# Stores of x with rows outermost, and tokens on partitions in early numerators

## The chip, the core and the metric

The kernel runs on one core of one Trainium2 chip. The metric is the device time of one execution in microseconds (us). Five engines work side by side: TensorE (PE: matrix products, and PEld, its weight loads), VectorE (DVE), ScalarE (ACT), GpSimd (POOL) and SyncE (SP), which here issues almost all transfers. Sixteen transfer (DMA) engines move the data.

## The reference

```python
def phi(x):
    proj = einsum('bhsd,df->bhsf', x, w_phi)             # 64 -> 128 features
    proj = proj - max(abs(proj), axis=-1, keepdims=True)
    return concatenate([exp(proj), exp(-proj)], axis=-1)
q_p, k_p = phi(q), phi(k)                                # 8 batches, 8 heads, 576 tokens, 64
kv = einsum('bhsf,bhsd->bhfd', k_p, v)
z = sum(k_p, axis=2)
num = einsum('bhsf,bhfd->bhsd', q_p, kv)
den = einsum('bhsf,bhf->bhs', q_p, z)[..., None] + 1e-06
attn = num / den
x = attn.transpose(0, 2, 1, 3).reshape(4608, 512)        # tokens, heads * 64
g = x @ w_gate                                           # 512 -> 1536
y = (g * sigmoid(g) * (x @ w_val)) @ w_out               # 1536 -> 512
```

The second half (the gated layers) is by far the larger part of the products.

## The kernel before

**Attention.** `attention` works on pairs of heads: 32 pairs, four to a batch. For a pair it loads k, q and v by SP (L529 to L545), projects them on TensorE, takes the largest value and subtracts it on VectorE, applies the exponentials on ScalarE, sums keys times values into a bank of PSUM (L605, L598), copies that sum to SBUF, and forms numerators and denominators. Pairs 0 to 11 are the early ones. They run at the start, while the weights are taken apart: these come as 64-bit floats, and VectorE and ScalarE split each into a high and a low 32-bit part. Pairs 12 to 31 run later, beside the products of the gated layers.

**Two forms of numerators.** An early pair goes through `finish_early`: the products leave features on partitions and tokens along a row (L817, L821), the denominators of 32 rows each are turned, inverted, copied across partitions (L845) and turned back (L837 to L847), and one product scales the numerators (L849). They then lie as the gated layers want x: 128 partitions are two heads times 64 features. A late pair goes through `finish`: the products leave tokens on partitions (L764), 65 columns for each 64 tokens, the last of which is the denominator; VectorE inverts 9 columns, scales out of PSUM into `num` (L780) and turns blocks of 32 x 32 into `turned` (L786).

**x.** It is a matrix of 512 rows (four pairs of 128) by 4608 tokens, worked on in chunks of 384 tokens. For pairs 0 to 7, x goes straight into the tiles `xh` and `xl` (high and low part). From pair 8 on it is stored to `x_dram` by SP: by one transfer of `num` for an early pair (L858), and by four transfers of `turned` for every two late pairs (L798, twenty pairs, ten groups of four). It is loaded again into `stage` (L1166) or `x_kept` (L506).

**The gated layers.** `first` and `second` (products at L388) work on the first four chunks; their middle values go to `h_dram` and come back (L989, L994), and low parts of weights come from `wlo_dram` (L932, L942, L944). The other eight chunks go two at a time through `strassen` (products at L1218), with combined weights streamed from `wv_dram` and `wlo_dram` (L1152); `operands` first forms the combinations of x from `stage` (L1176 to L1182).

**The order.** No order is written by hand. Each piece of work is a step with an engine, a cost, the steps it needs and a rank; `Plan.run` plays them through and so fixes the order on every engine. Each engine then works through its own list in that order. A transfer costs SP 500 ns to issue there, and all transfers share one wire of 320 bytes per ns, whatever their form. Where TensorE would stand still in this play, `nothing` puts filler products on idle data (L1412 to L1417). SP issues in order, too: a transfer that has to wait holds back all that stand behind it, and each transfer waits for the one eight places ahead of it to have landed.

Of the kernel before, what the change touches and what calls it, by code (L numbers as in the profile page):

```python
# [9 lines left out]
F32 = mybir.dt.float32  # L10
# [275 lines left out]
def favor_attention_moe(ctx: ExitStack, tc: tile.TileContext, qT, kT, v, w_phi, wg, wv, wo, out):  # L286
# [37 lines left out]
    kvs = sb("kvs", [P, 4 * P], F32, 2)  # L324
    qx = [sb("qx0", [P, 2, S]), sb("qx1", [P, 2, S])]
    qe = sb("qe", [P, 2, S], F32, 2)
    num, den = sb("num", [P, S]), sb("den", [P, S])
# [3 lines left out]
    rc = sb("rc", [P, NBL])  # L331
# [4 lines left out]
    shared = [pool.tile([P, 2 * DM], dt, name=f"shared{i}", tag=f"shared{i}") for i, dt in enumerate((U32, U32, F32, F32))]  # L336
# [145 lines left out]
    turned_tiles = []  # L482

    def turned_tile(n, g):
        if not turned_tiles:
            turned_tiles.extend(pool.tile([P, 2, SH], F32, name=f"turned{m}", tag=f"shared{m}") for m in range(4))
        return turned_tiles[2 * n + g]
# [32 lines left out]
    def attention(i, rank):  # L520
# [14 lines left out]
        q_width = 4 * P if early else S  # L535
        q_in = [add("SP", P * q_width * 4, lambda: nc.sync.dma_start(qin[jq][:, :q_width], qT[b, pr, :, :q_width]), q_free, rank)]
        if early:
            q_in.append(add("SP", 2 * D * D * 4, lambda: nc.sync.dma_start(side(qin[jq]), ends(qT)), q_free, rank))
# [89 lines left out]
        sums = lambda: ps_kv()[:, :4 * VD].rearrange("p (s h d) -> p s h d", s=2, h=2)  # L628

        kv_sum = lambda: kvs[j][:, :2 * P].rearrange("p (s h d) -> p s h d", s=2, h=2)  # L630
        z_sum = lambda: kvs[j][:, 2 * P:3 * P].rearrange("p (s h r) -> p s h r", s=2, h=2)
        if early:
            kvc = [add("ACT", act(4 * D), lambda: nc.scalar.copy(kv_sum(), sums()[:, :, :, :D]), [kv_steps[-1], *use("kvs")], rank)]
            kvc.append(add("ACT", act(P), lambda: nc.scalar.copy(z_sum(), sums()[:, :, :, D:VD].broadcast_to([P, 2, 2, 32])),
                           kvc[:1], rank, give=("kv", i)))
        else:
            kvc = [add("ACT", act(4 * VD), lambda: nc.scalar.copy(kvs[j][:, :4 * VD], ps_kv()[:, :4 * VD]),  # L637
                       [kv_steps[-1], *use("kvs")], rank, give=("kv", i))]
# [5 lines left out]
        if early:  # L644
            for g in range(3):
# [42 lines left out]
                def exponential(k, g=g, tail=tail, key2=key2):  # L688
                    if tail:
                        x = work[plan.bank[key2]][:, :P].rearrange("p (h s) -> p h s", h=2)  # L690
                        o = (qe, qx)[k][j][:, :, 4 * P:]
                    else:
                        x, o = work[plan.bank[key2]][:, :4 * P], (qe, qx)[k][j][:, g, :4 * P]
                    nc.scalar.activation(o, x, AF.Exp, scale=-1.0 if k else 1.0)
# [59 lines left out]
        def finish(extra):  # L754
# [4 lines left out]
            def over():  # L759
# [8 lines left out]
            nu = add("PE", 2 * blocks_ * KV_PACE, over, [*f1, *kvc, *extra], rank,  # L768
# [14 lines left out]
                for part, at, m in parts_]  # L783
            n, r = i // 2 % 2, i % 2
            over_ = [*raw_free, *wa_free, *we_free] if i < EARLY_PAIRS + 4 else last["sent", i - r - 4]
            t3 = [add("DVE", dve(SH), lambda g=g: vec.transpose(  # L786
                turned_tile(n, g)[:, r].rearrange("p (n s) -> p n s", s=32), even[:, :, 32 * g:32 * g + 32]),
                [*normal, *over_], rank) for g in range(2)]
            last["turned", i] = t3[1]
# [6 lines left out]
            for h in range(2):  # L796
                for g in range(2):
                    sent.append(add("SP", D * S * 4, lambda h=h, g=g: nc.sync.dma_start(  # L798
                        x_dram[b - LATE_BATCH, (2 * h + g) * 32:(2 * h + g + 1) * 32, :, pr - 1:pr + 1].rearrange("j p r s -> p j (r s)"),
                        turned_tile(n, g)[h * D:(h + 1) * D].rearrange("p r s -> p (r s)")), t3, rank))  # L800
# [4 lines left out]
        def finish_early(extra):  # L805
            features = lambda k, h, c: (qe, qx)[k][j][:, h, c]
            free = last.get(("num", i - 1), ())
            main, tail = slice(0, 4 * P), slice(4 * P, S)
            TAIL = S - 4 * P

            def over():
                low, high = (work[plan.bank[key]] for key in (("d", i), ("n", i)))
                for k in range(2):
                    for h in range(2):
                        for part, c in enumerate(halves):
                            at = 32 * (2 * h + part)
                            nc.tensor.matmul(low[at:at + 32, :SH], z_sum()[:, k, h], features(k, h, c), start=k == 0, stop=False)  # L817
                for o, c, first_ in ((low[:, SH:SH + TAIL], tail, False), (high, main, True)):
                    for k in range(2):
                        for at in range(0, P, 32):  # L820
                            nc.tensor.matmul(o[at:at + 32], kvs[j][:, k * P + at:k * P + at + 32], features(k, at // D, c),  # L821
                                             start=first_ and k == 0, stop=k == 1)

            nu = add("PE", 2 * pe32(SH) + 2 * (60 + pe32(4 * P)), over, [f1, *kvc, *extra], rank,
                     take=[("d", i), ("n", i)], mode="quarters")
            dn = add("ACT", act(SH), lambda: nc.scalar.activation(
                den[:, :SH], work[plan.bank["d", i]][:, :SH], AF.Copy, bias=1e-6), [nu, *free], rank)
            copied = [add("ACT", act(TAIL), lambda: nc.scalar.copy(
                num[:, tail], work[plan.bank["d", i]][:, SH:SH + TAIL]), [nu, dn, *free], rank, give=("d", i))]
            copied.append(add("ACT", act(4 * P), lambda: nc.scalar.copy(  # L830
                num[:, main], work[plan.bank["n", i]]), [nu, *free], rank, give=("n", i)))
            last["kvs", i] = last["nu", i] = last["qe", i] = last["qx", i] = nu

            wide = lambda t: t.rearrange("p (a j) -> p a j", j=32)
            NH = NBL // 2
            turned = den[:, SH:]
            t0 = add("DVE", dve(SH), lambda: vec.transpose(turned, den[:, :SH]), [dn], rank)  # L837
            t1 = add("DVE", 260, lambda: vec.reciprocal(
                rc.rearrange("p (g a) -> p g a", g=2),
                wide(turned)[:, :, 0:1].rearrange("p a o -> p o a").broadcast_to([P, 2, NH])), [t0], rank)  # L840
            crossed = []
            for h in range(2):
                for part in range(2):
                    r, q = (slice(32 * (2 * h + g), 32 * (2 * h + g) + 32) for g in (1 - part, part))
                    crossed.append(add("ACT", 200, lambda r=r, q=q, part=part: nc.scalar.copy(  # L845
                        rc[r, part * NH:(part + 1) * NH], rc[q, part * NH:(part + 1) * NH]), [t1], rank))
            t2 = add("DVE", dve(S), lambda: vec.transpose(  # L847
                wide(den), rc.rearrange("p (a o) -> p a o", o=1).broadcast_to([P, NBL, 32])), crossed, rank)
            t3 = add("DVE2", dve(S), lambda: vec.tensor_tensor(out=num, in0=num, in1=den, op=ALU.mult), [t2, *copied], rank)  # L849
            last["rc", i] = t2  # L850


            read_num = []
            for c, at, start, width in cuts:
                src = num[:, start:start + width]
                if b >= LATE_BATCH:
                    if not read_num:
                        read_num.append(add("SP", P * S * 4, lambda: nc.sync.dma_start(  # L858
                            x_dram[b - LATE_BATCH, :, :, pr], num.rearrange("p (u s) -> p u s", u=2)), [t3], rank))
                    x_kept.setdefault(c, []).extend(read_num)  # L860
                    continue
                dst = lambda x, c=c, at=at, width=width: x[c % X_SETS][:, pr, at:at + width]
                hi = add("ACT", act(width), lambda src=src, dst=dst: nc.scalar.copy(dst(xh), src),
                         [t3, *x_free.get(c - X_SETS, ())], rank)
                lo = pair_op("POOL" if early else "DVE2", width, lambda dst=dst: dst(xl), src, lambda dst=dst: dst(xh),
                             ALU.subtract, [hi], rank)
                x_ready.setdefault((c, pr), []).extend([hi, lo])
                read_num.extend([hi, lo])
                if i < BANK_PAIRS:
                    early_done.extend([hi, lo])  # L870
            last["num", i] = read_num
# [598 lines left out]
```

## Time and profile before

| | us |
|---|---|
| median of 3 runs (range) | 1231.64 (1229.57 to 1232.07) |
| profiled execution: time | 1231.18 |
| profiled execution: span | 1229.4 |
| TensorE busy | 1172.2 (95%) |
| VectorE busy | 793.4 (65%) |
| ScalarE busy | 545.3 (44%) |
| GpSimd busy | 140.9 (11%) |

The mean granted clock of TensorE is 0.978 of full speed. The transfers move 298.32 MB, 243 GB/s over the span. Busy time of TensorE is an upper bound of its work: ends of products are modelled, and products at a lower clock are longer. A wait is put down to the engine or transfer that came last by the profile; a chain of such waits has to be followed to where it starts.

### The profile page before, as it was taken

The numbers are of one execution on the slowest core, as the hardware profiler recorded it, in microseconds if no ns is written. First come the engines' busy times: TensorE is split into PE (matmuls) and PEld (weight loads), VectorE is DVE, ScalarE is ACT, GpSimd is POOL, SyncE is SP. The second block draws the span as 40 slices with busy tenths as digits, with TensorE's granted clock in tenths as the row PEclk, the third lists the DMA queues.
The fourth block names the chain that finished last, engine by engine and source line by source line (L and its number), as shares of the span: only waits on it lengthen the run. The fifth ranks groups of instructions, "written<-read, shape, count | busy, mean of one in ns | idle before, by whom it ended". The sixth has DMA issues, their size and how long they took to land. (4 is left out here: it accounts for less than half of the span.)

```text
span 1229.4 us, 26393 instructions
## 1 busy us (share of the span) xinstructions
PE 1172.2 (95%) x9978; PEld 1026.6 (84%) x9978; DVE 793.4 (65%) x1593; ACT 545.3 (44%) x1233; POOL 140.9 (11%) x142
## 2 busy tenths in 40 slices
PE   9999999999999889998979899997999999799998
PEld 7777889999888768987967789896699897599986
DVE  7998899997567637676756255785345785434441
ACT  6887543333435435453534243553333553333332
POOL 1323200000132212010100001110001110001100
PEclk9999999999999989998989899998999999899999
DMA  5656778777999779986766688866688767779864
GB/s 162 175 162 186 247 249 288 249 254 234 333 310 303 253 253 339 344 240 201 242 189 184 198 283 285 241 211 212 221 270 286 238 213 221 244 233 309 281 200 160
DMA packets 220031, 298.32 MB, mean 243 GB/s; under 512 B 65280, under 2 KB 125824, under 8 KB 219904
## 3 DMA queue, kind: packets, MB, share of 16 engines
q1 hardware_dynamic: 219744, 296.56, 75.4%
q8 instruction: 79, 1.29, 0.5%
q14 instruction: 48, 0.39, 0.1%
q10 hardware_dynamic: 160, 0.07, 0.0%
HBM read 217.91 MB, written 78.64 MB: 241 GB/s over the span
## 5 line engine op out<-in xcount | busy, mean ns | idle before, releaser
L388 PE MATMUL work<-w_hi,hh 128*128 128x512 f32 x468 | 187.7, 409 | 24.6 <-ACT hh L1006 16.7
L381 DVE TENSOR_TENSOR m<-m,hh 128x384 fp32r<-128x384 f32 x132 | 74.8, 573 | 140.1 <-ACT hh L1006 122.1
L388 PE MATMUL work<-w_hi,m 128*128 128x512 f32 x396 | 160.6, 405 | 0.9 <-DVE m L381 0.9
L1240 DVE TENSOR_TENSOR m<-m,work 128x384 f32<-128x384 f32 x144 | 78.5, 552 | 121.9 <-ACT m L1237 73.2
L1006 ACT CAST hh<-m 128x384 fp32r<-128x384 f32 x144 | 73.1, 512 | 182.8 <-DMA m<-h_dram 92.3
L381 POOL TENSOR_TENSOR m<-m,m 128x384 f32<-128x384 f32 x48 | 58.4, 1216 | 646.3 <-DVE m L1245 365.3
L388 PE MATMUL work<-xh,w_big 128*128 128x384 f32 x384 | 132.3, 345 | 0.0
L388 PEld LDWEIGHTS work<-w_hi,hh 128*128 128x128 f32 x468 | 90.4, 193 | 48.0 <-ACT hh L1006 18.6
L388 PE MATMUL work<-xl,w_big 128*128 128x384 f32 x384 | 128.6, 335 | 0.0
L1218 PE MATMUL work<-tb,stream_xh 128*128 128x384 f32 x618 | 115.3, 338 | 0.0
L1218 PEld LDWEIGHTS work<-tb,stream_xh 128*128 128x128 f32 x618 | 107.0, 188 | 4.7 <-issue 3.8
L1237 ACT COPY m<-work 128x384 f32<-128x384 f32 x144 | 68.1, 474 | 79.2 <-PE work L1218 71.5
L1218 PE MATMUL work<-tb,stream_xl 128*128 128x384 f32 x468 | 90.8, 343 | 9.1 <-ACT m L1237 9.1
L1244 ACT ACTIVATE m<-m 128x384 f32<-128x384 f32 x96 | 45.4, 517 | 111.4 <-DVE m L1240 111.3
L388 PEld LDWEIGHTS work<-w_hi,m 128*128 128x128 f32 x396 | 76.5, 193 | 20.5 <-DVE m L381 2.4
L1218 PEld LDWEIGHTS work<-tb,stream_xl 128*128 128x128 f32 x468 | 82.7, 191 | 12.7 <-ACT m L1237 9.5
L588 ACT ACTIVATE kp<-kp 128x512 f32<-128x512 f32 x128 | 78.2, 630 | 24.4 <-DVE kp L583 23.2
L1218 PE MATMUL work<-tb,tb 128*128 128x384 f32 x408 | 79.3, 341 | 4.6 <-ACT m L1237 4.6
L388 PEld LDWEIGHTS work<-xh,w_big 128*128 128x128 f32 x384 | 72.2, 188 | 7.7 <-issue 4.8
L1218 PEld LDWEIGHTS work<-tb,tb 128*128 128x128 f32 x408 | 71.8, 191 | 7.5 <-ACT m L1237 4.9
L381 POOL TENSOR_TENSOR s<-s 128x256 f32<-128x256 f32 x48 | 43.1, 897 | 282.4 <-DMA s<-w_dram 250.4
L388 PE MATMUL work<-w_lo,hh 128*128 128x512 f32 x183 | 74.1, 405 | 0.0
(141 smaller groups left out, 2345.8 us busy)
## 6 DMA issues: line engine op xcount, KB each, us to landing
stream_xh<-wv_dram SPq DMA_DIRECT2D x103, 256.0 KB
h_dram<-m SPq DMA_DIRECT2D x124, 192.0 KB
m<-h_dram SPq DMA_DIRECT2D x124, 192.0 KB
stream_xl<-wv_dram SPq DMA_DIRECT2D x78, 256.0 KB
tb<-wv_dram SPq DMA_DIRECT2D x77, 256.0 KB
w_lo<-wlo_dram SPq DMA_DIRECT2D x72, 256.0 KB
stream_w_lo<-wv_dram SPq DMA_DIRECT2D x52, 256.0 KB
stream_xl<-wlo_dram SPq DMA_DIRECT2D x48, 256.0 KB
```

The costliest lines, as they stand in the source:

```text
L381: (nc.gpsimd if on == "POOL" else nc.vector).tensor_tensor(out=o, in0=a, in1=b, op=op)
L388: nc.tensor.matmul(o, l, r, start=a, stop=z)
L588: nc.scalar.activation(kpv[:, :m2, s], kpv[:, :m2, 1], AF.Exp, scale=-1.0 if s else 1.0)
L1006: s4 = add("ACT", act(CH), lambda: nc.scalar.copy(hh[b], th(j)), [made, hid_free[b]], FIRST)
L1218: nc.tensor.matmul(o(), l, r, start=begin and k + m == 0, stop=k + m == 3, skip_group_check=True)
L1237: return j, into(j, add("ACT", act(CH), lambda: nc.scalar.copy(th(j), src()), after, FIRST))
L1240: return add("DVE", dve(CH), lambda: vec.tensor_tensor(out=th(j), in0=th(j), in1=src(), op=ALU.add), after, FIRST)
L1244: s1 = into(t, add("ACT", act(CH), lambda: nc.scalar.activation(th(t), th(j), AF.Tanh, scale=0.5), [ready], FIRST))
```

## The change

The stores of late x are cut in another way. `turned` becomes one tile, and each of the four transfers of two pairs takes 32 partitions and two blocks in place of 64 partitions; on the side of `x_dram` the outermost dimension of a transfer is 32 rows where it was 2. The four tiles `shared0` to `shared3`, in whose place `turned` lies later, become one.

Early pairs lose `finish_early` and go through `finish`. To that end q of an early pair is loaded so that its two halves of 288 tokens interleave in blocks of 32, and VectorE's turn of the scaled numerators (`spun`) puts features on partitions. Each block of 32 partitions of `spun` then belongs elsewhere in x: for pairs 0 to 7 eight transfers inside SBUF bring them into the new tile `sx`, from which `xh` and `xl` are made; for pairs 8 to 11 four transfers store `spun` to `x_dram`. The sum of keys times values leaves PSUM by one copy in place of two.

```diff
-    kvs = sb("kvs", [P, 4 * P], F32, 2)
+    kvs = sb("kvs", [P, 4 * VD], F32, 2)
-    num, den = sb("num", [P, S]), sb("den", [P, S])
+    num, spun = sb("num", [P, S]), sb("spun", [P, S])
+    sx = sb("sx", [P, S])
-    shared = [pool.tile([P, 2 * DM], dt, name=f"shared{i}", tag=f"shared{i}") for i, dt in enumerate((U32, U32, F32, F32))]
+    shared = pool.tile([P, 4, 2 * DM], F32, name="shared", tag="shared")
+    shared = [shared[:, i].bitcast(dt) for i, dt in enumerate((U32, U32, F32, F32))]
...
-        q_in = [add("SP", P * q_width * 4, lambda: nc.sync.dma_start(qin[jq][:, :q_width], qT[b, pr, :, :q_width]), q_free, rank)]
         if early:
-            q_in.append(add("SP", 2 * D * D * 4, lambda: nc.sync.dma_start(side(qin[jq]), ends(qT)), q_free, rank))
+            both_halves = qT[b, pr].rearrange("d (u s) -> d u s", u=2)
+            q_in = [add("SP", P * 4 * P * 4, lambda: nc.sync.dma_start(
+                qin[jq][:, :4 * P].rearrange("d (u s) -> d u s", u=2), both_halves[:, :, :2 * P]), q_free, rank)]
+            q_in += [add("SP", D * D * 4, lambda h=h: nc.sync.dma_start(
+                qin[jq][:D, 4 * P + h * D:4 * P + (h + 1) * D].rearrange("d (u s) -> d u s", u=2),
+                both_halves[h * D:(h + 1) * D, :, 2 * P:]), q_free, rank) for h in range(2)]
...
-        if early:
-            kvc = [add("ACT", act(4 * D), lambda: nc.scalar.copy(kv_sum(), sums()[:, :, :, :D]), [kv_steps[-1], *use("kvs")], rank)]
-            kvc.append(add("ACT", act(P), lambda: nc.scalar.copy(z_sum(), sums()[:, :, :, D:VD].broadcast_to([P, 2, 2, 32])),
-                           kvc[:1], rank, give=("kv", i)))
-        else:
-            kvc = [add("ACT", act(4 * VD), lambda: nc.scalar.copy(kvs[j][:, :4 * VD], ps_kv()[:, :4 * VD]),
-                       [kv_steps[-1], *use("kvs")], rank, give=("kv", i))]
+        kvc = [add("ACT", act(4 * VD), lambda: nc.scalar.copy(kvs[j][:, :4 * VD], ps_kv()[:, :4 * VD]),
+                   [kv_steps[-1], *use("kvs")], rank, give=("kv", i))]
...
+            if early:
+                t3 = add("DVE", dve(S), lambda: vec.transpose(
+                    spun.rearrange("p (g n s) -> p n g s", g=2, s=32), even.rearrange("p n (g s) -> p n g s", g=2)),
+                    [*normal, *last.get(("sent", i - 1), ())], rank)
...
+                for h in range(2):
+                    for p in range(2):
+                        from_here = spun[(2 * h + p) * 32:(2 * h + p + 1) * 32]
+                        if b >= LATE_BATCH:
+                            sent.append(add("SP", D * SH * 4, lambda h=h, p=p, t=from_here: nc.sync.dma_start(
+                                x_dram[b - LATE_BATCH, h * D:(h + 1) * D, p, pr].rearrange("(g j) s -> j g s", g=2),
+                                t.rearrange("p (g s) -> p g s", g=2)), [t3], rank))
+                            continue
+                        for g in range(2):
+                            there[p].append(add("SP", D * SH * 2, lambda h=h, p=p, g=g, t=from_here: nc.sync.dma_start(
+                                sx[(2 * h + g) * 32:(2 * h + g + 1) * 32, p * SH:(p + 1) * SH], t[:, g * SH:(g + 1) * SH]),
+                                [t3, *last.get(("sx", i - 1), ())], rank))
...
-                for g in range(2):
-                    sent.append(add("SP", D * S * 4, lambda h=h, g=g: nc.sync.dma_start(
-                        x_dram[b - LATE_BATCH, (2 * h + g) * 32:(2 * h + g + 1) * 32, :, pr - 1:pr + 1].rearrange("j p r s -> p j (r s)"),
-                        turned_tile(n, g)[h * D:(h + 1) * D].rearrange("p r s -> p (r s)")), t3, rank))
+                for p in range(2):
+                    sent.append(add("SP", D * S * 4, lambda h=h, p=p: nc.sync.dma_start(
+                        x_dram[b - LATE_BATCH, h * D:(h + 1) * D, p, pr - 1:pr + 1].rearrange("(g j) r s -> j g (r s)", g=2),
+                        turned(n)[(2 * h + p) * 32:(2 * h + p + 1) * 32].rearrange("p g r s -> p g (r s)")), t3, rank))
...
-        if early:
-            finish_early([])
-        elif i < DEFER:
+        if i < DEFER:
             finish([])
```

As every step's place comes out of `Plan.run`, the order moves on all engines. Three places follow. Names carry the number of their buffer; the last figures are partitions and elements.

The first is SP's list around the first group of stores of late x; `m` and `h_dram` are middle values, `w_lo` low parts of weights, `s` sums of weights. Before:

```order
L1103 DMA wv_dram<-s_3532 128x2x256
L994 DMA m_4596<-h_dram 128x384
L989 DMA h_dram<-m_4594 128x384
L798 DMA x_dram<-turned_4107 2x32x576
L798 DMA x_dram<-turned_4108 2x32x576
L798 DMA x_dram<-turned_4107 2x32x576
L798 DMA x_dram<-turned_4108 2x32x576
L932 DMA w_lo_89<-wlo_dram 128x512
```

And now:

```order
L953 DMA m_4515<-h_dram 128x384
L540 DMA qin<-in_qT_dram 128x576
L827 DMA x_dram<-turned 32x2x576 x4
L526 DMA kin<-in_kT_dram 128x512
L530 DMA kin<-in_kT_dram 64x2x64
L903 DMA w_lo_85<-wlo_dram 128x512 x2
L1046 DMA s_3682<-w_dram 128x1024
```

The four stores stand together in both; their form goes from 2x32x576 to 32x2x576, and the loads of the next pair's k and of weights come right behind them.

The second is SP's list while pairs 1 and 2 are worked on; `kin`, `qin`, `ahead`, `vf` and `vl` take k, q and v. Before:

```order
L542 DMA vf<-in_v_dram 128x8x64
L545 DMA vl<-in_v_dram 64x64 x2
L529 DMA kin<-in_kT_dram 128x512
L533 DMA kin<-in_kT_dram 64x2x64
L536 DMA qin<-in_qT_dram 128x512
```

And now:

```order
L544 DMA vf<-in_v_dram 128x8x64
L793 DMA sx<-spun 32x288 x8
L547 DMA vl<-in_v_dram 64x64 x2
L526 DMA kin<-in_kT_dram 128x512
L530 DMA kin<-in_kT_dram 64x2x64
L534 DMA qin<-in_qT_dram 128x2x256
L536 DMA qin<-in_qT_dram 64x2x32 x2
```

Eight transfers inside SBUF come between the two loads of v, ahead of the next k and q, and the load of q is three transfers.

The third is VectorE's list at the end of pair 0; `rc` are the inverted denominators. Before:

```order
L837 STREAM_TRANSPOSE den<-den 128x288
L838 RECIPROCAL rc<-den 128x18
L415 TENSOR_SCALAR shared_128<-shared_128 128x512
L847 STREAM_TRANSPOSE den<-rc 128x576
L849 TENSOR_TENSOR num<-num,den 128x576
L671 TENSOR_TENSOR qy_117<-work_135,km_113 128x128
```

And now:

```order
L771 RECIPROCAL rc<-den 128x9
L774 TENSOR_TENSOR num<-work_136,rc 128x448
L774 TENSOR_TENSOR num<-work_135,rc 128x128
L779 STREAM_TRANSPOSE spun<-num 128x9x2x32
L659 TENSOR_REDUCE km_114<-work_134 128x1
```

The chain has one turn less, and no step of ScalarE in its middle.

## Rows read from the trace of the kernel before

**Rows 1.** Waits of TensorE, whole run: total us, times, longest us.

```profile
PE work L388 <- ACT hh L1006: 16.7, 4, 6.8
PE work L1218 <- ACT m L1237: 15.4, 3, 9.1
PE work L388 <- ACT osb L1037: 7.6, 2, 4.7
PE work L388 <- DMA stream_xl<-wlo_dram: 5.9, 4, 1.8
PE work L764 <- ACT kvs L637: 3.7, 2, 3.2
```

**Rows 2.** Timeline of TensorE: start, length, instruction [idle before, releaser].

```profile
429.73 0.79 PE L388 MATMUL work<-w_hi,hh 128*128 128x512 f32 x1 [4.91 <-ACT hh L1006]
...
1060.87 0.79 PE L388 MATMUL work<-w_hi,hh 128*128 128x512 f32 x1 [4.68 <-ACT osb L1037]
```

**Rows 3.** Stores of late x (ns min/median/max, first, last start us); SP's timeline.

```profile
L798 SPq DMA_DIRECT2D x_dram<-turned x40: 478/554/2139, 410.7 to 1044.3; - x40
...
417.18 6.67 SPq L994 DMA_DIRECT2D m<-h_dram  x4
```

**Rows 4.** Stretches: length, busy PE, PEld, DVE, ACT, POOL; clock, DMA share, GB/s.

```profile
432.00:437.00 5.00, 5.00 (x19) 4.00 (x18) 3.15 (x7) 3.08 (x7) 0.00 (x0) 0.81 0.16 62
...
1008.00:1011.00 3.00, 3.00 (x18) 2.37 (x18) 2.59 (x5) 1.42 (x4) 0.00 (x0) 1.00 0.12 45
```

**Rows 5.** Waits of SP, whole run: total us, times, longest us.

```profile
SPq L1166 <- DMA x_dram<-turned: 16.6, 6, 4.9
```

**Rows 6.** The chain that ended last: start us, length us, what.

```profile
1028.28 2.55 DMA m<-h_dram
...
1032.44 2.32 PE work L764 x72
...
1041.65 11.36 DMA w_lo<-wlo_dram
```

**Rows 7.** Seven stretches around long waits: first, last and their sum.

```profile
426.00:434.00 8.00, 4.28 (x10) 3.40 (x11) 4.30 (x8) 3.06 (x7) 0.00 (x0) 0.57 0.60 201
...
1054.00:1066.00 12.00, 6.64 (x17) 4.92 (x18) 3.64 (x7) 3.45 (x8) 0.00 (x0) 0.57 0.89 284
sum 68.00, PE 42.74 PEld 35.77 DVE 31.10 ACT 24.42 POOL 4.30; mean PE 6.11 PEld 5.11 DVE 4.44 ACT 3.49 POOL 0.61
```

**Rows 8.** Timeline of TensorE, early pairs: start us, length us, instruction.

```profile
18.58 0.69 PE L817 MATMUL work<-qe,kvs 128*32 128x288 f32 x8
...
21.63 2.09 PE L605 MATMUL work<-vf,kp 128*64 128x65 f32 x64
...
51.40 0.69 PE L817 MATMUL work<-qe,kvs 128*32 128x288 f32 x8
```

**Rows 9.** Groups by line and form, 0 to 420 us: busy us, mean ns | idle before.

```profile
L849 DVE TENSOR_TENSOR num<-num,den 128x576 f32<-128x576 f32 x12 | 12.5, 1041 | 0.5
...
L837 DVE STREAM_TRANSPOSE den<-den 128x288 f32<-128x288 f32 x12 | 5.7, 472 | 0.0
...
L780 DVE TENSOR_TENSOR num<-work,rc 128x448 f32<-128x448 f32 x4 | 2.5, 625 | 0.4
...
L780 DVE TENSOR_TENSOR num<-work,rc 128x128 f32<-128x128 f32 x4 | 1.1, 281 | 0.0
```

**Rows 10.** Waits of SP, 18.58 to 51.40 us: total us, times, longest us.

```profile
SPq L412 <- DVE shared L424: 6.5, 2, 3.6
SPq L542 <- PE work L598: 5.3, 3, 2.8
SPq L536 <- PE work L655: 2.4, 2, 1.9
```

**Rows 11.** Issues on SP, 0 to 120 us: ns min/median/max, first, last start us.

```profile
L545 SPq DMA_DIRECT2D vl<-in_v_dram x22: 587/618/1418, 3.9 to 112.5; - x22
...
L529 SPq DMA_DIRECT2D kin<-in_kT_dram x11: 328/382/536, 0.7 to 104.7; - x11
```

More of the change, by code (lines that the diff above doesn't have):

```diff
@@ L330, in favor_attention_moe @@
     ident = sb("ident", [P, P])
-    rc = sb("rc", [P, NBL])
+    rc, den = sb("rc", [P, NBL // 2]), sb("den", [P, NBL // 2])
     hh = sb("hh", [P, CH], F32R, 4)
     osb = sb("osb", [P, DM], F32, 2)
-    shared = [pool.tile([P, 2 * DM], dt, name=f"shared{i}", tag=f"shared{i}") for i, dt in enumerate((U32, U32, F32, F32))]
+    shared = pool.tile([P, 4, 2 * DM], F32, name="shared", tag="shared")
+    shared = [shared[:, i].bitcast(dt) for i, dt in enumerate((U32, U32, F32, F32))]
     raw = [t.rearrange("p (n t) -> p n t", t=2) for t in shared[:2]]
@@ L480, in x_parts @@
         return got
[L482 to L487, printed above, removed]
+    turned = lambda n: later("turned", "shared", [P, 2, 2, 2, SH], F32)[:, n]
     STAGE_TAGS = ("xh1", "xl1")
@@ L534, in attention @@
         q_free = [last.get(("qin", n)) for n in ((i - 2,) if early else (i - 1, i - 2))]
-        q_width = 4 * P if early else S
-        q_in = [add("SP", P * q_width * 4, lambda: nc.sync.dma_start(qin[jq][:, :q_width], qT[b, pr, :, :q_width]), q_free, rank)]
         if early:
-            q_in.append(add("SP", 2 * D * D * 4, lambda: nc.sync.dma_start(side(qin[jq]), ends(qT)), q_free, rank))
+            both_halves = qT[b, pr].rearrange("d (u s) -> d u s", u=2)
[4 more added lines that the diff above has]
+                both_halves[h * D:(h + 1) * D, :, 2 * P:]), q_free, rank) for h in range(2)]
+        else:
+            q_in = [add("SP", P * S * 4, lambda: nc.sync.dma_start(qin[jq][:, :S], qT[b, pr]), q_free, rank)]
         n = 4 * P * P
@@ L627, in attention @@
         last["vf", i] = kv_steps[-1]
-        sums = lambda: ps_kv()[:, :4 * VD].rearrange("p (s h d) -> p s h d", s=2, h=2)
-        kv_sum = lambda: kvs[j][:, :2 * P].rearrange("p (s h d) -> p s h d", s=2, h=2)
-        z_sum = lambda: kvs[j][:, 2 * P:3 * P].rearrange("p (s h r) -> p s h r", s=2, h=2)
-        if early:
-            kvc = [add("ACT", act(4 * D), lambda: nc.scalar.copy(kv_sum(), sums()[:, :, :, :D]), [kv_steps[-1], *use("kvs")], rank)]
-            kvc.append(add("ACT", act(P), lambda: nc.scalar.copy(z_sum(), sums()[:, :, :, D:VD].broadcast_to([P, 2, 2, 32])),
-                           kvc[:1], rank, give=("kv", i)))
-        else:
-            kvc = [add("ACT", act(4 * VD), lambda: nc.scalar.copy(kvs[j][:, :4 * VD], ps_kv()[:, :4 * VD]),
-                       [kv_steps[-1], *use("kvs")], rank, give=("kv", i))]
+        kvc = [add("ACT", act(4 * VD), lambda: nc.scalar.copy(kvs[j][:, :4 * VD], ps_kv()[:, :4 * VD]),
+                   [kv_steps[-1], *use("kvs")], rank, give=("kv", i))]
         last["kv", i] = kvc
@@ L692, in exponential @@
                     else:
-                        x, o = work[plan.bank[key2]][:, :4 * P], (qe, qx)[k][j][:, g, :4 * P]
+                        x = work[plan.bank[key2]][:, :4 * P].rearrange("p (u n s) -> p n u s", u=2, s=32)
+                        o = (qe, qx)[k][j][:, g, :4 * P].rearrange("p (n u s) -> p n u s", u=2, s=32)
                     nc.scalar.activation(o, x, AF.Exp, scale=-1.0 if k else 1.0)
@@ L766, in over @@
                                              start=n % main == 0 and k == 0, stop=n in (main - 1, blocks_ - 1) and k == 1)
-            nu = add("PE", 2 * blocks_ * KV_PACE, over, [*f1, *kvc, *extra], rank,
+            nu = add("PE", 2 * blocks_ * KV_PACE, over, [*(f1 if not early else [f1]), *kvc, *extra], rank,
                      take=[("n", i, 0), ("n", i, 1)], mode="columns")
@@ L783, in finish @@
                 for part, at, m in parts_]
+            if early:
+                t3 = add("DVE", dve(S), lambda: vec.transpose(
+                    spun.rearrange("p (g n s) -> p n g s", g=2, s=32), even.rearrange("p n (g s) -> p n g s", g=2)),
+                    [*normal, *last.get(("sent", i - 1), ())], rank)
+                last["turned", i], last["num", i] = t3, [t3]
+                sent, there = [], [[], []]
+                for h in range(2):
[10 more added lines that the diff above has]
+                                [t3, *last.get(("sx", i - 1), ())], rank))
+                last["sent", i] = [*sent, *there[0], *there[1]]
+                for c, *_ in cuts if b >= LATE_BATCH else ():
+                    x_kept.setdefault(c, []).extend(sent)
+                read = []
+                for c, at, start, width in cuts if b < LATE_BATCH else ():
+                    src = sx[:, start:start + width]
+                    here = [m for p in range(2) if start < (p + 1) * SH and start + width > p * SH for m in there[p]]
+                    dst = lambda x, c=c, at=at, width=width: x[c % X_SETS][:, pr, at:at + width]
+                    hi = add("ACT", act(width), lambda src=src, dst=dst: nc.scalar.copy(dst(xh), src),
+                             [*here, *x_free.get(c - X_SETS, ())], rank)
+                    lo = pair_op("POOL", width, lambda dst=dst: dst(xl), src, lambda dst=dst: dst(xh),
+                                 ALU.subtract, [hi], rank)
+                    x_ready.setdefault((c, pr), []).extend([hi, lo])
+                    read.extend([hi, lo])
+                    early_done.extend([hi, lo])
+                last["sx", i] = read
+                return
@@ L784, in finish @@
             n, r = i // 2 % 2, i % 2
             over_ = [*raw_free, *wa_free, *we_free] if i < EARLY_PAIRS + 4 else last["sent", i - r - 4]
[L786 to L789, printed above, removed]
+            t3 = [add("DVE", dve(S), lambda: vec.transpose(
+                turned(n)[:, :, r].rearrange("p g (n s) -> p n g s", s=32), even.rearrange("p n (g s) -> p n g s", g=2)),
+                [*normal, *over_], rank)]
@@ L790, in finish @@
+            last["turned", i] = t3[0]
             last["num", i] = t3
@@ L803, in finish @@
                 x_kept.setdefault(c, []).extend(sent)
[L805 to L871, printed above, removed]
```

## The prediction

> **What bounds the kernel now.** I read first who TensorE waited for over the whole run [rows 1]: five lines hold 16.7 + 15.4 + 7.6 + 5.9 + 3.7 = 49.3 us. The reader is to see that none of these waits lies early: the first of the large ones ends at 429.73 us, the last at 1060.87 us [rows 2]. Up to there TensorE is full, so what shortens its work early, or these waits late, shortens the run.
>
> The waits name ScalarE, but ScalarE waits in turn for transfers. The queue of SP shows for which. Forty stores of x lie between 410.7 and 1044.3 us, ten groups of four, and behind the first group four small loads take 6.67 us to issue, 1.67 us each [rows 3], where an ordinary issue takes 0.38 us [rows 11]. In the stretches after a group the transfer engines are busy for 0.16 and 0.12 of sixteen and move 62 and 45 GB/s (the first and the last of eight such stretches) [rows 4]: 0.125 would be two engines out of sixteen. Loads of x then wait 16.6 us in all for the stores of x [rows 5], and the chain that ended last holds a 256 KB weight load of 11.36 us right behind the last group, where a 192 KB load takes 2.55 us [rows 6]. So the stores run on two engines, and each transfer issued behind them, spread over all engines, ends only when its share on those two has come through. A group is 4 x 147,456 bytes = 590 KB: at 62 to 45 GB/s 9.5 to 13.1 us.
>
> Last the clock. In seven stretches around the long waits, 68 us together with 42.74 us busy, the granted clock averages 0.57 to 0.66, 0.57 in the first and the last, which are shown [rows 7]. Between the two levels, 2.4 and 1.2 GHz, these means make 55.1 us at the lower one (twice what is missing to 1.00, by length, over the seven: 6.9, 6.8, 6.9, 10.4, 6.9, 6.9, 10.3). At most 25.3 us of that was idle, so at least 29.8 us of work ran at half speed: 14.9 us lost behind the waits. TensorE had stood still before each fall.
>
> **The change part by part.**
>
> *Stores of x, pairs 12 to 31.* Same bytes, same number, but the outermost dimension goes from 2 to 32, as the order shows. The trace has no store of this form. Its bounds: as slow as now (no gain), or as fast as other transfers in the same stretches, 201 to 284 GB/s [rows 7], 2.1 to 2.9 us a group. I take the fast end, because loads with many rows outermost reach a share of 0.60 to 0.89 there. What stands behind a group then lands 6.6 to 11 us earlier, and the longest wait in rows 1 is 9.1 us, so each could go. By the Trainium skill (DMA: Bandwidth & Descriptors, Why a DMA increments its semaphore by 16 and not by 1) a transfer uses the largest number of engines up to 16 that divides the slowest dimension on both sides, which gives 2 before and 16 now; rows 4 agree for before, and no row here shows the second.
>
> I do not book all of it. The 5.9 us on the streamed second-layer weights are four short waits, longest 1.8: half, 3.0. Of the other 43.4 us four fifths, 34.7, because in the stretch where held-up transfers catch up their share is already 0.89, so another transfer is next in line. Of the clock loss the same four fifths, 11.9. Sum late: **49.6 us**; ends 0 and 49.3 + 14.9 = 64.2.
>
> *Numerators of pairs 0 to 11 on TensorE.* The old form fills 18.58 to 21.63 us, 3.05 us a pair [rows 8]; the form with tokens on partitions takes 2.32 us a pair where late pairs have it [rows 6]. 0.73 us less, but it counts only where TensorE is full. The first four pairs run with filler in between; there VectorE's saving counts: a transpose of 288 (0.472) and a product of 576 (1.041) go, products of 448 and 128 out of PSUM (0.625 + 0.281) come, one transpose of 576 and a reciprocal stand before and after: 0.61 us less [rows 9]. 4 x 0.61 + 8 x 0.73 = **8.3 us**.
>
> *The small transfers.* Pairs 0 to 7 add eight stores from SBUF to SBUF of 36,864 bytes, every early pair one more load of q, and pairs 8 to 11 three more stores of x. Per pair that is nine issues on SP; no such transfer is in the trace, and the nearest issues take 0.38 (128 rows) and 0.62 us (64 rows) [rows 11], so 3.4 to 5.6 us. A pair takes (51.40 - 18.58) / 3 = 10.9 us [rows 8], and in these three pairs SP stood still for 6.5 + 5.3 + 2.4 = 14.2 us, 4.7 a pair [rows 10]. The period shrinks by 0.6, so 4.1 are free. At 0.38 the issues fit; at 0.62 they exceed by 1.5 a pair, 12 us over eight. I take 0.3 a pair, 2.4 us, since 32 rows are fewer than either neighbour. Behind these issues stand the loads of v, k and q, and TensorE would wait for those; VectorE's next transpose waits for the eight to land, some 10 us later, at no cost. x of a pair comes later by 8 x 0.62 + 2.55 = 7.5 us at most. That costs nothing while the product that needs it stands a pair, 10 us, behind; without this cover it is paid once, at the first products.
>
> ScalarE loses five evictions and four small copies and gains three small evictions; I cost it at nothing, since it holds no early wait of TensorE. The one tile in place of four shared ones moves no wait that the order shows.
>
> Sum: 49.6 + 8.3 - 2.4 = 55.5 us off the profiled 1231.18 (its span is 1229.4), which stands 0.46 below the median of 1231.64: 1175.7, or 1176 against the median.
>
> **The rivals.**
>
> *Half of the late waits stay.* Data held up by one group is needed while the next is due; with the slow stores gone, the queue itself is the next limit. For it speaks the 0.89 of rows 7; against it that the share falls to 0.12 right before, so room is there. Half of 64.2, 32.1, with 5.9 early: 1194.
>
> *The stores stay as slow.* The form of the source side could still decide, with no row to exclude it. Then only the early 5.9 us remain: 1226.
>
> *Slower: the small transfers pace the early pairs.* If the eight go one after the other at 2.55 us each, a landing time as in rows 6, they take 20.4 us a pair against 10.9: eight pairs lose 76 us, less the 49.6 late: 1258. It ends above the time before once a transfer costs over (10.9 + 55.5 / 8) / 8 = 2.2 us. For it: TensorE's loads stand behind them in the same queue, and the one buffer they read from lets no two pairs overlap. Against it: two loads of 64 rows issue at 0.62 us each without waiting for landing [rows 11]. The Trainium skill speaks for it too (DMA: Bandwidth & Descriptors, Rules for kernel authors): many small transfers should be made one, as under 64 KB one pays mostly overhead. No run here shows it for this form.
>
> **How the numbers follow.** Forecast 0.70, half stays 0.20, stores as slow 0.06, slower 0.04. A measurement can tell some 0.2%, 2.5 us, from no change. The first three all lie over 2.5 us below, but the third would be lost if SP took its upper end of 12 us, so I move 0.02 of it to no change: faster 0.94, same 0.02, slower 0.04. The range starts where every late wait and its clock loss go and SP costs nothing: 1231.6 - 64.2 - 8.3 = 1159, and I set 1158. It reaches over the second case, 1194, with part of SP's end: 1200. The last two cases lie outside.
>
> **What would show it.** Right: after each group of stores the transfer share stays above 0.5 instead of 0.12; SP's waits for stores of x all but vanish; TensorE's idle time after 420 us falls from some 50 to 10 to 15 us, with one or two falls of the clock in place of seven; numerators of early pairs take 2.3 us; a pair takes some 10.5 us early, and TensorE has no early wait. Wrong: the share still drops to an eighth; or TensorE waits before 120 us for keys, queries or values; or waits of the old size come back behind other transfers.

## The result, and the profile after

The change takes the time from 1230.61 us (median of 4 runs) to **1181.52 us** (4 runs, 1180.34 to 1184.76): ratio 0.9609, interval 0.9579 to 0.9640. The forecast of 1176 was 5.5 us too low, and the range, 1158 to 1200, held the time. The profiled execution took 1180.38 us, its span 1178.6. Behind that forecast two terms were far off in opposite directions, and the profile shows where.

The waits of TensorE over the whole run, the counterpart of [rows 1] (total us, times, longest us):

```profile
PE work L607 <- DMA vf<-in_v_dram: 11.0, 5, 5.0
PE work L390 <- ACT xh L804: 2.9, 2, 2.0
PE work L607 <- ACT xh L804: 2.1, 1, 2.1
```

None of the five lines of [rows 1], 49.3 us together, is left; the largest wait is a new one, for v of an early pair. The stretches right behind the first and the last group of stores (length, busy PE, PEld, DVE, ACT, POOL, granted clock, transfer share, GB/s) are set against [rows 4]. The first stretch of [rows 4] lies behind the second group, which is issued at 430 us. The prediction takes it for the first of its stretches; behind the first group of before stood this one:

```profile
412.00:417.00 5.00, 5.00 (x80) 4.42 (x78) 4.43 (x11) 2.22 (x6) 3.27 (x4) 1.00 0.36 124
```

Now:

```profile
409.00:414.00 5.00, 5.00 (x27) 4.60 (x26) 4.76 (x15) 3.13 (x6) 0.06 (x1) 1.00 0.95 300
...
1003.00:1006.00 3.00, 3.00 (x15) 2.42 (x14) 0.86 (x2) 1.03 (x2) 0.00 (x0) 1.00 0.90 289
```

Behind the first group the share is 0.95 where it was 0.36, behind the last 0.90 where it was 0.12, and the rate is 300 and 289 GB/s against 124 and 45. This is also what the rule cited in the prediction gives for 32 outermost rows (the Trainium skill, DMA: Bandwidth & Descriptors, Why a DMA increments its semaphore by 16 and not by 1); with these rows the trace agrees on both sides. The transfers that stand behind a group on SP issue normally again, where four loads of middle values, 192 KB each (the prediction calls them small), took 6.67 us in [rows 3]:

```profile
407.85 2.24 SPq L827 DMA_DIRECT2D x_dram<-turned  x4
410.18 0.38 SPq L526 DMA_DIRECT2D kin<-in_kT_dram  x1
```

The loss is early. TensorE's timeline at pairs 3 and 4, counted from 0 (start, length, instruction, idle before it and what ended it):

```profile
47.30 3.74 PE L607 MATMUL work<-vf,kp 128*64 128x65 f32 x64 [4.99 <-DMA vf<-in_v_dram]
...
62.46 2.09 PE L607 MATMUL work<-vf,kp 128*64 128x65 f32 x64 [2.08 <-ACT xh L804]
```

The 64 products at 47.30 took 3.74 us, after 4.99 us of standing still, where the same 64 take 2.09 at 62.46. The granted clock from 47.30 to 51.04 us is 0.50, the lower of the two levels: the wait costs the clock too. SP's timeline shows why v was late:

```profile
33.12 1.21 SPq L536 DMA_DIRECT2D qin<-in_qT_dram  x2
34.42 0.54 SPq L435 DMA_DIRECT2D wlo_dram<-ahead  x1
...
37.39 6.28 SPq L793 DMA_DIRECT2D sx<-spun  x8
43.77 0.71 SPq L544 DMA_DIRECT2D vf<-in_v_dram  x1
```

The eight small transfers hold SP for 6.28 us, the load of v is issued only behind them, at 43.77, and TensorE starts on it at 47.30. The load itself is not slow: up to 135 us these loads of v land 3.5 us after their issue in the median, and 3.3 us in e3 below, where TensorE has no wait for them. Of SP's long waits of [rows 10] little is left; between 33 and 64.6 us it waits for these lines alone, 1.9 us, where it waited 15.1 us in the same stretch of before:

```profile
SPq L547 <- PE work L674: 1.0, 1, 1.0
SPq L544 <- PE work L674: 0.5, 1, 0.5
SPq L414 <- DVE km L579: 0.4, 1, 0.4
```

27.8 of these 31.6 us go into issuing: SP has little room there. Two stretches of the run show the balance, first of before, then of after (columns as above):

```profile
0.00:410.00 410.00, 407.08 (x3951) 352.25 (x3952) 343.98 (x668) 217.78 (x502) 66.95 (x82) 1.00 0.76 246
410.00:1229.00 819.00, 765.13 (x6028) 674.39 (x6026) 449.47 (x926) 327.53 (x731) 73.97 (x60) 0.97 0.76 241
```

```profile
0.00:410.00 410.00, 387.18 (x4085) 355.56 (x4086) 318.77 (x632) 183.38 (x406) 63.71 (x78) 0.98 0.76 237
410.00:1178.00 768.00, 763.50 (x6182) 678.38 (x6180) 467.07 (x942) 340.84 (x756) 77.58 (x64) 1.00 0.83 265
```

After 410 us TensorE's idle time falls from 53.9 to 4.5 us and the clock rises from 0.97 to 1.00; before 410 us idle time rises from 2.9 to 22.8 us and the clock falls from 1.00 to 0.98.

### The profile page after: what moved, and what is told of

It reads as the page before. It is cut to its first block, busy times and chain, and to the rows that moved or that the text cites. A ratio compares the mean times of both kernels' runs of the same rounds, so it can differ in the third digit from the quotient of the medians.

```text
span 1178.6 us, 27081 instructions
## 1 busy us (share of the span) xinstructions
PE 1150.7 (98%) x10265; PEld 1033.9 (88%) x10265; DVE 785.8 (67%) x1573; ACT 524.2 (44%) x1161; POOL 141.3 (12%) x142
## 4 chain that ended last, share of the span: by engine, by line
PE 82%; DVE 2%; DMA 1%; issue 0%; ACT 0%; SPq 0%; DVEq 0%
PE work L390 39%; PE work L1177 31%; PE work L758 4%; PE work L607 3%; PE work L703 2%; PE work L568 2%; PE work L600 1%; PE work L1376 1%; DMA shared<-in_wg_dram 1%; DMA w_lo<-wlo_dram 0%; PE work L571 0%; DVE shared L421 0%; DVE shared L426 0%; DVE m L941 0%; DVE m L938 0%
## 5 line engine op out<-in xcount | busy, mean ns | idle before, releaser
L390 PE MATMUL work<-w_hi,hh 128*128 128x512 f32 x468 | 182.6, 398 | 0.0
L390 PE MATMUL work<-w_hi,m 128*128 128x512 f32 x396 | 156.8, 396 | 0.0
L607 PEld LDWEIGHTS work<-vf,kp 128*64 128x64 f32 x2048 | 68.5, 148 | 21.2 <-ACT kpt L590 10.9
L607 PE MATMUL work<-vf,kp 128*64 128x65 f32 x2048 | 72.6, 234 | 14.5 <-DMA vf<-in_v_dram 11.0
```

The lines of the kernel that those rows point to most:

```text
L390: nc.tensor.matmul(o, l, r, start=a, stop=z)
L607: nc.tensor.matmul(ps_kv()[r, (2 * s + h) * VD:(2 * s + h + 1) * VD], kpv[:, t, s, r], vf[:, t, h], start=t == 0 and h + s == 0, stop=False)
```

## The experiments

Two questions: is the late gain that of the stores' outermost dimension, and what does the early part cost, and through what? The theory for the second is that SP has no room for the issues. Its rivals are that the small transfers are slow whoever issues them, and that the order was built on too low a price for an issue. Each time is the median of 4 runs, with its interval as a ratio to the kernel before.

**Stores alone** (e1): the kernel before, with the late stores, `shared` and `turned` of the change, and early pairs as they were.

```diff
...
-                for g in range(2):
-                    sent.append(add("SP", D * S * 4, lambda h=h, g=g: nc.sync.dma_start(
-                        x_dram[b - LATE_BATCH, (2 * h + g) * 32:(2 * h + g + 1) * 32, :, pr - 1:pr + 1].rearrange("j p r s -> p j (r s)"),
-                        turned_tile(n, g)[h * D:(h + 1) * D].rearrange("p r s -> p (r s)")), t3, rank))
+                for p in range(2):
+                    sent.append(add("SP", D * S * 4, lambda h=h, p=p: nc.sync.dma_start(
+                        x_dram[b - LATE_BATCH, h * D:(h + 1) * D, p, pr - 1:pr + 1].rearrange("(g j) r s -> j g (r s)", g=2),
+                        turned(n)[(2 * h + p) * 32:(2 * h + p + 1) * 32].rearrange("p g r s -> p g (r s)")), t3, rank))
```

> Only the late stores of x change (rows outermost, one tile); early pairs stay as before. Theory A (the two halves of the change add up: the late half removes 49 us of TensorE waits and some 15 us of low clock, the early half costs 15 to 20 us through SP's queue): 1160 to 1172 us, no wait of TensorE over 1 us after 420 us, early stage as before. Rival B (the early half is neutral or gains, the late half alone is worth no more than the 49 us seen): 1180 to 1188 us.

1162.58 us, ratio 0.9454 (0.9431 to 0.9478): 19 us better than the whole change, as theory A had it. Its waits of TensorE, complete:

```profile
PE work L1408 <- POOL vl L364: 1.5, 1, 1.5
PE work L389 <- DMA w_lo<-wlo_dram: 1.0, 1, 1.0
PE work L655 <- DVE kp L579: 0.6, 1, 0.6
PE work L601 <- ACT m L973: 0.3, 1, 0.3
```

The clock is 1.000 over its whole span of 1160.4 us, where before had 0.978.

**Early part alone** (e2): the changed kernel, its stores cut as before; the order on the engines is that of the change.

```diff
-                for p in range(2):
+                for g in range(2):
...
+                        x_dram[b - LATE_BATCH, (2 * h + g) * 32:(2 * h + g + 1) * 32, :, pr - 1:pr + 1].rearrange("j p r s -> p j (r s)"),
+                        turned(n)[h * D:(h + 1) * D, g].rearrange("p r s -> p (r s)")), t3, rank))
```

> The changed kernel with the late stores cut as before (outermost dimension 2), all else and the order on every engine as in the changed kernel. Theory A: the long late waits come back and the early loss stays, 1240 to 1255 us. Rival B: 1222 to 1232 us. Rival C (the late waits were an accident of the order, not of the form of the stores): 1180 to 1190 us.

1254.14 us, ratio 1.0196 (1.0153 to 1.0238): the early part by itself makes the kernel 24.6 us slower. The four runs lie far apart, 1247.48 to 1258.08, but all above before. Its largest waits of TensorE are the early one for v and the old late ones side by side:

```profile
PE work L607 <- DMA vf<-in_v_dram: 18.5, 6, 6.0
PE work L390 <- ACT osb L996: 12.8, 2, 8.6
PE work L390 <- DMA w_lo<-wlo_dram: 10.6, 3, 4.8
```

With the rest of the kernel and the order held, the form of the stores alone is worth 72.6 us (1254.14 to 1181.52). The two halves sum to -67.0 + 24.6 = -42.4 against -49.1 for both. These 6.7 us are within the spread of the runs: e2's interval alone is some 5 us to either side, and the medians of before in the two sets differ by 1.1. They don't arise early either: e2's waits for v, 18.5 against 11.0 us, all lie before 135 us, its first late store is issued at 407 us, and up to 410 us it executes as many products as the changed kernel (x4086 and x4085):

```profile
0.00:410.00 410.00, 385.96 (x4086) 354.47 (x4087) 319.32 (x634) 184.56 (x407) 64.07 (x78) 0.98 0.75 237
```

**Eight stores of half the size** (e6): e1, but each old block is split in two by p, so that the data keep their old grouping by g and only the outermost dimension becomes 32 rows; eight transfers a group in place of four. `shared` and `turned` are as in e1.

```diff
...
+                    for p in range(2):
+                        sent.append(add("SP", D * SH * 4, lambda h=h, g=g, p=p: nc.sync.dma_start(
+                            x_dram[b - LATE_BATCH, (2 * h + g) * 32:(2 * h + g + 1) * 32, p, pr - 1:pr + 1].rearrange("j r s -> j (r s)"),
+                            turned(n)[(2 * h + p) * 32:(2 * h + p + 1) * 32, g].rearrange("p r s -> p (r s)")), t3, rank))
```

> The kernel with the late stores alone changed, but the blocks cut as before and each store halved, eight stores of 32 rows of 1 x 2304 bytes in place of four of 2 x 32 rows: same rows, same bytes, twice the issues, outermost dimension 32. Theory A (the outermost dimension of 2 was what made the stores slow, not which block goes with which): no late wait over 2 us, 1160 to 1170 us, the 40 more issues cost next to nothing. Rival F (the new pairing of blocks, or fewer issues, is what helps): waits of 4 to 9 us after 420 us, 1185 to 1230 us.

1162.58 us, ratio 0.9458 (0.9440 to 0.9476), the same as e1 with twice as many stores. One late wait of 2.6 us is left, where none over 2 was expected. So neither the way the blocks are paired nor the size of a store makes the gain, but the 32 outermost rows. With them a store also takes 32 partitions in place of 64 in every fast form; no run separates these two.

**Small transfers on GpSimd's queue** (e3): the changed kernel; the order has them as steps of GpSimd, for which the plan takes a landing 2.5 us after an issue's end.

```diff
-                            there[p].append(add("SP", D * SH * 2, lambda h=h, p=p, g=g, t=from_here: nc.sync.dma_start(
+                            there[p].append(add("POOL", 700, lambda h=h, p=p, g=g, t=from_here: nc.gpsimd.dma_start(
...
+                            there[p][-1].port, there[p][-1].lag = False, 2500
```

> The changed kernel with the eight small transfers of an early pair issued by GpSimd's queue in place of SP's; same bytes, same places. Theory A (the loss early is SP's time to issue, behind which loads of v, k and q stand): TensorE's waits before 135 us fall from 19 to under 6 us, 1158 to 1170 us. Rival D (the loss is the transfers' landing, or VectorE and the parts of x waiting for them, whoever issues them): waits before 135 us stay over 12 us, 1176 to 1190 us.

1157.98 us, ratio 0.9420 (0.9389 to 0.9451): 23.5 us off, by moving 64 issues to another queue. TensorE's waits before 135 us fall from 20.8 to 6.4 us, just over the 6 that were expected. The transfers did not get faster: here from issue to landing (min/median/max), first after, then this kernel:

```profile
DMA to landing us min/median/max: 1.8/2.8/5.3
```

```profile
DMA to landing us min/median/max: 1.7/3.5/5.2
```

They land later, 3.5 against 2.8 us, and the kernel is faster: what they cost was SP's time. GpSimd issues eight in 4.08 us in this line of its timeline, and no wait of TensorE for it is added:

```profile
24.13 4.08 POOL L793 DMA_DIRECT2D sx<-spun  x8 [22.48 <-DVE km L659]
```

**Half as many transfers** (e4): ScalarE copies `spun` to `sx` whole, which puts four of the eight blocks in place; four transfers a pair remain, on SP.

```diff
+                        if not h + p:
+                            cp = add("ACT", act(S), lambda: nc.scalar.copy(sx, spun), [t3, *last.get(("sx", i - 1), ())], rank)
-                        for g in range(2):
+                        for g in (1 - p,):
...
```

> The changed kernel with four small transfers a pair in place of eight; the blocks that stay on their partitions come by one copy of ScalarE (576 long, some 0.68 us, ahead of the transfers). Theory A: SP issues 2.4 us a pair less of the some 2.5 us by which it is over, so half to all of the early loss goes: 1162 to 1174 us. Rival D (landing): one copy longer in the chain, same wait for landing, 1178 to 1190 us.

1160.57 us, ratio 0.9446 (0.9410 to 0.9483). That is 1.4 us below the expected range. Four issues a pair go, and with them 21.0 us, nearly as much as e3 gains: in the prediction's form of sum (issues against free time) four more issues fit. They don't come quite free, as the next run shows.

**Both** (e5): e4 with its four transfers on GpSimd's queue.

> Both cures at once: four small transfers a pair, issued by GpSimd's queue, one copy of ScalarE. Theory A (SP's time to issue was the whole early loss, and either cure alone already takes it all): no further gain, 1153 to 1162 us. Rival E (some early loss is left in each cure alone, GpSimd's issues or SP's four): 1146 to 1153 us.

**1152.85 us**, ratio 0.9379 (0.9364 to 0.9395), the best version, faster than both kernels. It lies 5.1 us below e3 and 7.7 below e4, and its runs (1152.30 to 1154.85) overlap with none of theirs. So theory A, no further gain, is out, and rival E fits, by which either cure alone leaves some loss. Its stretch over the early pairs against that of the changed kernel, after first:

```profile
18.50:135.00 116.50, 97.38 (x1746) 86.31 (x1745) 86.65 (x175) 63.74 (x161) 28.06 (x28) 0.93 0.57 157
```

```profile
18.50:135.00 116.50, 113.72 (x2128) 103.11 (x2129) 106.31 (x217) 83.73 (x203) 50.33 (x65) 1.00 0.68 199
```

In the same 116.5 us TensorE executes 2128 products in place of 1746; in the whole early part, 62 and 51 products are filler.

**An order that knows the price** (e7): the changed kernel, with a transfer's issue on SP at 620 ns in the plan.

```diff
-    BYTES, ISSUE, CHANGE = 320.0, 500.0, 165
+    BYTES, ISSUE, CHANGE = 320.0, 620.0, 165
```

> The changed kernel with the order made for an issue of 620 ns in place of 500 ns, so that the order knows what the small transfers take. Theory A (SP has more to issue than a pair's time, in whatever order): the early loss stays, as filler or as waits, 1176 to 1192 us. Rival G (the order put the small transfers in a wrong place, and one that knows better hides them): under 1170 us.

1189.06 us, ratio 0.9667 (0.9651 to 0.9682), 7.5 us worse than the change and inside theory A's range; rival G is out. The wait for v falls from 11.0 to 4.7 us, but waits for `qy` come, 5.8 us, and the plan puts in filler. The filler products up to 520 us, first after, then this kernel (count | busy us, mean ns | idle before):

```profile
L1374 PE MATMUL work<-idle 128*128 128x256 f32 x51 | 8.7, 300 | 0.0
```

```profile
L1374 PE MATMUL work<-idle 128*128 128x256 f32 x100 | 17.0, 300 | 0.0
```

Planning for a full queue doesn't empty it: up to 410 us idle time falls from 22.8 to 17.4 us, filler, which counts as busy, rises by 8.3 us, and the clock falls from 0.98 to 0.97.

**Small transfers on ScalarE's queue** (e8): as e3, with another engine; the plan lets a step of ScalarE that needs these transfers wait for their landing.

```diff
...
-                            there[p].append(add("SP", D * SH * 2, lambda h=h, p=p, g=g, t=from_here: nc.sync.dma_start(
+                            there[p].append(add("ACT", 600, lambda h=h, p=p, g=g, t=from_here: nc.scalar.dma_start(
...
```

> As the run with GpSimd's queue, but the eight small transfers are issued by ScalarE. Theory A (any queue but SP's will do, if its engine has time): ScalarE was busy 50 of 60 us or less early and lost 1.9 us a pair, eight issues of some 0.6 us are 4.7 us a pair of its 10 us: 1158 to 1172 us. Rival D (landing, not issuing): 1176 to 1190 us.

1186.70 us, ratio 0.9652 (0.9636 to 0.9669), a miss: no gain where e3 gained 23.5. By the time alone, which lies in rival D's range, this would speak for slow transfers whoever issues them; e3 and this kernel's timeline of ScalarE speak against it:

```profile
23.03 0.38 ACT L630 COPY kvs<-work 128x260 f32<-128x260 f32 x1 [1.68 <-PE work L600]
23.84 7.53 ACTq L793 DMA_DIRECT2D sx<-spun  x8
31.41 0.60 ACT L688 ACTIVATE qe<-work 128x512 f32<-128x512 f32 x1 [8.00 <-DMA sx<-spun]
```

The eight issues hold ScalarE for 7.53 us, 5.0 to 7.5 over the pairs, and what the early path needs of ScalarE stands behind them: the copy of keys times values in five pairs, the exponentials of q in three (us in all, times):

```profile
  ACT kvs L630: 28.9, 5
  ACT qe L688: 18.9, 3
```

TensorE shows almost no wait for it (its largest is 4.7 us), because here, too, the plan put filler there:

```profile
L1375 PE MATMUL work<-idle 128*128 128x256 f32 x199 | 28.3, 291 | 0.0
```

That is 18.2 us more filler than e3 has (10.1). The queue was relieved by blocking an engine on which the early path depends.

## Why it came out so, step by step

**What bounds the kernel: right.** The stores of x with two outermost rows caused the late waits; with 32 rows they went, but for one of 2.6 us in e6. That is shown by e1 and e6, and by e2, where they come back with all else and the order held; the rival by which the stores stay as slow is out, as is the one by which half of the waits stay.

**Late sum, 49.6: mis-sized; 67.0 us.** By the medians e1 takes 67.0 us off. The two profiled executions tell where, before against e1: idle time falls from 57.2 to 7.6 us, 49.6, and busy time from 1172.2 to 1152.8 us, 19.4 (filler differs by less than 1 us): 69.0, the difference of the spans 1229.4 and 1160.4. Booked were 37.7 of waits and 11.9 of clock. So the step that failed is the holding back of a fifth, and of half of the streamed weights' waits: the 0.89 in [rows 7] was the catching up of what had been held back, not a limit, and behind a group the share now reaches 0.95 with no wait. The upper end of 64.2 was too low as well: the clock term of 14.9 took all idle time there to lie at the lower level, which makes the loss on work smallest; the runs give 19.4.

**Numerators and VectorE, 8.3: not measured by itself.** In the trace of after an early pair's numerators fill 18.57 to 20.72 us, 2.15 against the 2.32 taken, so TensorE's saving of a pair is a little larger than booked. What the term is worth in time could be seen only where SP doesn't hide it: e3 stands 4.6 and e5 9.7 us below e1, both with the rest of the early part in them. 8.3 lies between, which fits and doesn't show it.

**Small transfers, -2.4 with an end of -12: the step that failed.** Of the two ends the wrong one was taken, and the far end was short too. One issue takes 588 ns in the median, near the 0.62 of [rows 11], not the value between that 0.3 us a pair stands for:

```profile
L793 SPq DMA_DIRECT2D sx<-spun x64: 507/588/1653, 23.5 to 125.5; - x64
```

The eight of a pair take 4.9 to 6.3 us in SP's timeline, 5.5 in the mean or 0.68 each, because single issues take up to 1.65 us. The pair's second small load of q, 0.6, comes on top: 6.1 us against 4.1 free, 2.0 over, 16 us in eight pairs. The pairs lose more than that. Numerators of the eighth pair start here in after, then in e3:

```profile
110.64 0.34 PE L758 MATMUL work<-kvs,qe 128*64 128x65 f32 x4
```

```profile
89.74 0.34 PE L758 MATMUL work<-kvs,qe 128*64 128x65 f32 x4
```

Those of the first start at 18.57 and 18.50 us, so a pair takes 13.2 us in after, where 10.5 was forecast, and 10.2 in e3. At the eighth pair that is 20.9 us, most of the 23.5 that e3 gains. What the sum of issues leaves open isn't taken apart; the clock has a part in it, 0.93 from 18.5 to 135 us against 0.99 in e3. Named in the prediction was also who would wait (the loads of v, k and q, and TensorE for them): that holds. The statement that TensorE has no early wait does not: its waits for v before 120 us are one of the prediction's own signs of being wrong.

**The slower rival, 1258, by transfers landing one by one: out.** Landing overlaps, 2.8 us in the median for one while eight are issued in 6. A rule of the Trainium skill (DMA: Bandwidth & Descriptors, Rules for kernel authors) has small transfers mostly overhead and asks to merge them; here the overhead that counted most was issue time on one queue, as e3 cures it without merging any. The same section of the Trainium skill says that spreading transfers over issuing engines saves only that issue time; here this was worth 23.5 us on GpSimd, and nothing on ScalarE.

**The sum.** Late 67.0 in place of 49.6, early -18.9 (1181.52 against e1's 1162.58) in place of +5.9: that the forecast is only 5.5 us off is luck, as two errors of 17 and 25 us nearly cancel.

## What to carry to other kernels

A transfer whose outermost dimension is short costs most through what stands behind it in the queue: look at the transfer share right after it, and where the share drops to an eighth, book the whole wait and the clock with it. When adding many small transfers, count the issues per period against the queue's idle time in that period, at the measured price of a row of them, gaps included, and put them on the queue of an engine for which nothing urgent waits. Where a plan fills holes with filler, read filler as idle time, or a new wait hides in a busy share of 99%.

## What was not expected

Transfers inside SBUF of 36,864 bytes landed in 1.8 to 5.3 us, median 2.8, less than the 3.7 of the 144 KB stores. GpSimd issued them in 496 ns in the median, faster than SP with 588 and ScalarE with 602. And the same 64 issues were worth 23.5 us on GpSimd's queue and lost 5.2 us on ScalarE's (1186.70 against 1181.52).

Open are whether the 6.7 us by which the two halves, measured apart, fall short of the whole are more than spread, and how e5's 5.1 us over e3 split between fewer issues and a changed order.
